# Pooled attention and two feed-forward layers on one core: Float32 heads spread over the second batch, first loads in pieces, the fourth batch's sums inverted by DRAM

## The chip, the cores and the metric

The kernel runs on one core of one Trainium2 chip. The metric is the device time in microseconds (us), the median over runs. The profile is of one such execution and has its own time.

## What is computed

The queries of each of 4 batches and 8 heads (1152 rows of 64) are pooled in pairs, the softmax attention over 1152 keys is taken, and the result goes through two feed-forward layers.

```python
q_pool = q.reshape(B, H, S // factor, factor, D).mean(axis=3)
scores = scale * np.matmul(q_pool, k.transpose(0, 1, 3, 2))
attn = np.exp(scores - np.max(scores, axis=-1, keepdims=True))
attn = attn / (np.sum(attn, axis=-1, keepdims=True) + 1e-09)
x = np.matmul(attn, v)                   # then (tokens, 512)
h = np.maximum(x @ w_in, 0.0)            # first layer, d_ff 2048
x = (s * (h * h) + b) @ w_out
out = (1 / (1 + np.exp(-(x @ w_gate))) * (x @ w_val)) @ w_out2   # second, d_ff 1536
```

The weights arrive as float64 and are decoded on the chip. Matmul operands are split into a high and a low part of type fp32r, and each product is the sum of two or three matmuls of such parts.

## The kernel before

**A plan sets the order.** Every operation is added to a `Plan` (line 1700 on) with its engine, a duration, what it reads and writes, and a rank. `Plan.order` then issues, engine by engine, the free operation with the lowest rank. The rank is the operation's place in its stage, from the tables `ATTENTION` and `FEED`, and a correction from the table `MOVED`, by the operation's name, its pair and its batch. So the order of the instructions on each engine (PE, DVE, ACT, POOL) and of the DMA issues (SP) is fixed at build time, and a number in `MOVED` moves instructions. An engine runs its own list in that order. An operation that either of two engines may do (`shared`) goes to the one that the plan finds free.

**The stages.** For each batch the heads are taken in four pairs. `pair_prep` (L2378) loads q, k and v of a pair, adds the pooled rows of q (L2023), copies the sum beside itself (L2013 on ACT, L2015 on POOL), transposes q and k on PE (L2423), and writes the high parts on ACT (q L2443, k L2020) and the low parts on DVE (q L2446, k L2026). The first batch is done by rows (`pair_rows`): scoring matmuls of 384 keys (L2657), the row maximum of each on DVE (L2664) and of three of them (L2667), the exponential on ACT (L2671), transposes of the probabilities (L2702), and values times probabilities (L2724). The other batches go by half heads (`pair_half`): scoring matmuls (L2493), a running maximum on DVE, transposes of the maximum, a reduce to `mc` (L2510), transposes of that back into rows (L2467), the subtraction, the exponential, and values times probabilities.

**Values times probabilities.** A half head has three thirds of 864 columns. In most heads each third is split into a high and a low part (`split_p`: the high part a cast on ACT, L2013, or POOL, the low part a subtraction, L2023, on DVE or POOL). The heads listed in `WHOLE` (heads 0 to 3 of the second batch) skip the split and use Float32 matmuls (L2549) on the probabilities and values themselves.

**The sums.** Each half head pair needs the reciprocal of 2x288 sums. In `pair_half` (L2617) either the sums are spread to all 64 rows of each half and DVE inverts the 128x288 tile (L2628), or `inverse` writes one row per head to DRAM (L2604), reads it back as 64x9 (L2606), inverts that (L2607), and goes out and back by DRAM (L2608, L2612), all four DMAs on SP. The fourth batch and the last half of each batch's last pair take the first way.

**The feed-forward work of a batch** runs beside the attention of the next one: `ffn1` (`yy` and `xx` are split inputs; its matmuls are L2096 to L2098) and `ffn2`. Those of the fourth batch run at the end, alone. The weights are decoded during the first batch's feed-forward work (`raw`, L2043 to L2059) and fetched from DRAM later (L2073, L2078).

**The PSUM banks.** All PSUM tiles are one of 8 banks. An operation that writes a bank waits until its last reader is done.

Of the kernel before, what the change touches and what calls it, by code (L numbers as in the profile page):

```python
# [3018 lines left out]
```

## Time and profile before

| | |
|---|---|
| median of 3 runs | 1350.54 us (1350.36 to 1352.05) |
| the profiled execution's own time | 1351.29 us |
| its span, first to last instruction | 1349.5 us |
| PE busy | 1313.8 us (97%) |
| DVE busy | 1128.4 us (84%) |
| ACT busy | 903.6 us (67%) |
| POOL busy | 903.2 us (67%) |
| mean granted TensorE clock | 0.996 |

The span is read by engines: an engine's busy time is the time in which one of its instructions ran, and the rest of the span it waited. In a row of the timeline the bracket at the end gives the idle time before the row and what ended it. The granted clock is a share of full speed: 1.00 is the level of 2.4 GHz, 0.50 that of 1.2 GHz.

### The profile page before, as it was taken

The page shows a single profiled execution, that of the slowest core. Times are in us where ns is not written, and L with a number is a line of the kernel's source. Part 1 is how long each engine was busy: PE and PEld are TensorE (multiplying, and loading weights), DVE is VectorE, ACT ScalarE, POOL GpSimd, SP SyncE. Part 2 cuts the span into 40 slices and gives each one's busy share as a digit, 9 for nine tenths or more (in the row PEclk, how much of TensorE's full clock was granted, in tenths as well). Part 3 has the DMA queues.
Part 4 walks back from the last instruction along what each step waited for, and adds up shares of the span by engine and source line. Part 5 has one row for each costly group of instructions (what it writes and reads, how often), then busy time and mean ns, then how long its engine had stood idle before and what let it go on. Part 6 is the DMA issues. An engine that isn't in the chain of part 4 may idle for free.

```text
span 1349.5 us, 21795 instructions
## 1 busy us (share of the span) xinstructions
PE 1313.8 (97%) x7524; PEld 1169.8 (87%) x7524; DVE 1128.4 (84%) x1848; ACT 903.6 (67%) x1919; POOL 903.2 (67%) x767
## 2 busy tenths in 40 slices
PE   7999999998999999999999999999999999999998
PEld 6888888887888898888888888888888899999997
DVE  6899887998989998889989998898978646677675
ACT  6899977667888688768777667676855364343321
POOL 4578755657789876668868877586765455446562
PEclk9999999999999999999999999999999999999999
DMA  3246325876776764445343544343333434435332
GB/s 97 54 116 216 99 90 178 280 243 222 229 259 222 265 198 163 147 160 184 131 144 137 174 165 156 148 161 142 117 143 121 159 132 159 153 120 188 125 125 47
DMA packets 102373, 214.85 MB, mean 159 GB/s; under 512 B 49756, under 2 KB 72056, under 8 KB 86136
## 3 DMA queue, kind: packets, MB, share of 16 engines
q1 hardware_dynamic: 101096, 213.18, 47.4%
q8 instruction: 59, 0.97, 0.3%
q14 instruction: 50, 0.41, 0.1%
q10 hardware_dynamic: 1168, 0.29, 0.1%
HBM read 173.02 MB, written 40.43 MB: 158 GB/s over the span
## 4 chain that ended last, share of the span: by engine, by line
PE 78%; DVE 8%; ACT 6%; POOL 3%; DMA 3%; issue 2%; DVEq 0%; POOLq 0%; ACTq 0%
PE banks L2096 11%; PE banks L2098 11%; PE banks L2097 11%; PE banks L2493 6%; PE banks L2849 4%; PE banks L2851 4%; PE banks L2850 4%; PE banks L2567 3%; PE banks L2233 3%; PE banks L2235 3%; PE banks L2234 3%; PE banks L2559 2%; PE banks L2724 2%; PE banks L2549 2%; DVE st L2026 2%
## 5 line engine op out<-in xcount | busy, mean ns | idle before, releaser
L2026 DVE TENSOR_TENSOR st<-banks,st 128x288 f32<-128x288 f32 x384 | 171.9, 450 | 29.9 <-ACT st L2020 18.2
L2096 PE MATMUL banks<-xx,w 128*128 128x512 f32 x480 | 192.9, 402 | 0.9 <-DVE raw L2059 0.8
L2097 PE MATMUL banks<-xx,w 128*128 128x512 f32 x480 | 188.8, 393 | 0.0
L2098 PE MATMUL banks<-xx,w 128*128 128x512 f32 x480 | 188.8, 393 | 0.0
L2023 POOL TENSOR_TENSOR pp<-st,pp 128x864 fp32r<-128x864 f32 x76 | 173.3, 2285 | 12.2 <-ACT pp L2013 6.0
L2020 ACT COPY st<-banks 128x288 f32<-128x288 f32 x432 | 153.6, 407 | 40.8 <-PE banks L2493 29.9
L2493 PE MATMUL banks<-qT,kT 128*128 128x288 f32 x864 | 158.6, 303 | 2.5 <-DVE y L2340 1.1
L2026 DVE TENSOR_TENSOR st<-st,banks 128x864 f32<-128x864 f32 x144 | 148.2, 1043 | 4.3 <-PE banks L2467 3.9
L2493 PEld LDWEIGHTS banks<-qT,kT 128*128 128x128 f32 x864 | 134.3, 190 | 15.1 <-DVE st L2026 1.4
L2519 ACT ACTIVATE st<-st 128x864 f32<-128x864 f32 x144 | 132.7, 935 | 19.4 <-DVE st L2026 18.3
L2098 PEld LDWEIGHTS banks<-xx,w 128*128 128x128 f32 x480 | 90.5, 189 | 20.1
L2096 PEld LDWEIGHTS banks<-xx,w 128*128 128x128 f32 x480 | 90.7, 189 | 13.2 <-DVE raw L2059 1.0
L2097 PEld LDWEIGHTS banks<-xx,w 128*128 128x128 f32 x480 | 90.9, 189 | 10.8
L2013 ACT CAST pp<-st 128x864 fp32r<-128x864 f32 x102 | 93.4, 922 | 0.8 <-PE banks L2567 0.4
L2096 PE MATMUL banks<-g,w 128*128 128x512 f32 (+2 forms) x256 | 87.4, 342 | 0.0
L2097 PE MATMUL banks<-g,w 128*128 128x256 f32 (+1 forms) x256 | 86.5, 338 | 0.0
L2098 PE MATMUL banks<-g,w 128*128 128x512 f32 (+2 forms) x256 | 86.5, 338 | 0.0
L2023 POOL TENSOR_TENSOR g<-raw,g 128x512 fp32r<-128x512 f32 (+1 forms) x31 | 54.4, 1754 | 37.4 <-ACT g L2013 18.1
L2023 POOL TENSOR_TENSOR w<-raw,w 128x512 fp32r<-128x512 f32 x55 | 75.2, 1368 | 4.9 <-ACT w L2013 4.0
L2023 POOL TENSOR_TENSOR pp<-st,st 128x864 f32<-128x864 f32 x19 | 39.6, 2083 | 43.3 <-ACT st L2519 38.8
L2023 DVE TENSOR_TENSOR pp<-st,pp 128x864 fp32r<-128x864 f32 x44 | 65.6, 1490 | 2.9 <-PE banks L2559 1.1
L2567 PE MATMUL banks<-pp,vt 128*128 128x288 f32 x360 | 67.9, 297 | 0.0
(250 smaller groups left out, 3991.8 us busy)
## 6 DMA issues: line engine op xcount, KB each, us to landing
w<-d_2g_2v SPq DMA_DIRECT2D x26, 1024.0 KB
w<-d_1u_1u SPq DMA_DIRECT2D x24, 1024.0 KB
w<-d_1d_1d SPq DMA_DIRECT2D x24, 1024.0 KB
w<-d_2d_2d SPq DMA_DIRECT2D x18, 1024.0 KB
raw<-in_moe_w_out_dram SPq DMA_DIRECT2D x28, 512.0 KB
d_2g_2v<-w SPq DMA_DIRECT2D x12, 1024.0 KB
w<-d_2g_2v SPq DMA_DIRECT2D x20, 512.0 KB
qn<-in_q_dram SPq DMA_DIRECT2D x16, 576.0 KB
```

The lines of the kernel that those rows point to most:

```text
L2013: nc.scalar.copy(out=out(), in_=in_())
L2020: act(name, n, lambda: nc.scalar.copy(out=out(), in_=in_()), r, w, rank, sbuf=False)
L2023: shared(name, n, lambda e: ENGINE[e].tensor_tensor(out=out(), in0=in0(), in1=in1(), op=op), r, w, rank, 2.25)
L2026: dve(name, n, lambda: nc.vector.tensor_tensor(out=out(), in0=in0(), in1=in1(), op=op), r, w, rank)
L2096: nc.tensor.matmul(ps(), lhsT=whi(), rhs=xhi(), start=first, stop=False)
L2097: nc.tensor.matmul((ps_lo or ps)(), lhsT=whi(), rhs=xlo(), start=False, stop=False)
L2098: nc.tensor.matmul(ps(), lhsT=wlo(), rhs=xhi(), start=False, stop=last)
L2493: nc.tensor.matmul(ps.t[:, :HQ], lhsT=kT.t[:, c], rhs=qq[:, w, hf * HQ:(hf + 1) * HQ], start=(w == 0), stop=(w == 1))
L2519: act("exp", 3 * HQ, lambda s=s: nc.scalar.activation(out=s.t[:, :3], in_=s.t[:, :3], func=AF.Exp), [], parts, AT)
L2567: nc.tensor.matmul(acc.t[:, :HQ], lhsT=vt.t[:, 3 * i + c, cols], rhs=lo.t[:, c], start=False, stop=(i == c == 2))
L2849: nc.tensor.matmul(po.t, lhsT=hi, rhs=w.t[:, 0], start=(i == 0), stop=False)
L2850: nc.tensor.matmul(po.t, lhsT=hi, rhs=w.t[:, 1], start=False, stop=False)
```

## The change

Four parts:

- **Float32 heads.** `WHOLE` lists heads 0, 2, 4 and 6 of the second batch, not 0 to 3. The number of such heads stays 4.
- **First loads.** For the first pair alone, q comes in two loads (of 4 and 5 double rows) and each head's k in two (of 4 and 5 chunks). The first parts of both heads' k are issued by ACT, the rest by SP, q first. The pooled add and the copy beside it are made for each part. Ahead of all that PE gets 13 transposes of the identity (`warm`).
- **The fourth batch's sums.** All its half pairs but the last pair's two are inverted by DRAM.
- **The tables.** `ATTENTION`, `FEED` and nearly all numbers of `MOVED` are new, so instructions move on every engine.

```diff
-WHOLE = [(1, h) for h in range(4)]
+WHOLE = [(1, h) for h in range(0, 8, 2)]
...
-ATTENTION = (0.0, 158.683, 461.124, 811.569, 1195.188)
-FEED = ((143.971, 478.863), (483.888, 862.257), (845.806, 1213.263), (1049.765, 2170.948))
+ATTENTION = (0.0, 157.746, 450.031, 812.875, 1178.305)
+FEED = ((143.343, 476.347), (521.404, 861.584), (845.878, 1191.044), (992.951, 2301.912))
...
-    "q load": 72.917,
...
+    "warm": 94.003,
...
+        first = b == hp == 0
+
+        def warm(count, reads, writes):
+            pt = bank(tag)
+
+            def issue():
+                for i in range(count):
+                    nc.tensor.transpose(pt.t[:, i % 4 * P:(i % 4 + 1) * P], ident, ident)
+
+            pe("warm", count * 107, issue, reads, [pt, *writes], rq - 500)
+
+        if first:
+            warm(13, [], [])
+        rcuts, kcuts = ([(0, 4), (4, RQ)], [(0, 4), (4, NK)]) if first else ([(0, RQ)], [(0, NK)])
...
+        for i in range(len(rcuts)):
+            load_q(i)
+            for j in range(2):
+                load_k(i, j, nc.scalar if first and i == 0 else nc.sync)
...
-        last = b == B - 1 or hp == NP - 1 and hf == 1
+        last = hp == NP - 1 and (b == B - 1 or hf == 1)
```

The count of instructions stays: 7380 matmuls and transposes on PE before, 7393 with the 13 new ones. On DVE six reciprocals of 128x288 become six of 64x9, and SP has 30 more DMA issues for them.

**Where instructions move.** First, PE at the start of the program (`kn` and `qn` are the loaded k and q, `kT` and `qT` their transposed parts, `qm` the middle block of q, `st` the probabilities). Before:

```order
L2423 MATMUL banks<-ident,kn_179 128x128 x9
L2423 MATMUL banks<-ident,qn_182 128x128 x9
L2657 MATMUL banks<-kT_187,qT_208 128x384 x22
L2702 MATMUL banks<-ident,st_237 128x128
L2702 MATMUL banks<-ident,st_248 128x128
```

Changed:

```order
L2405 MATMUL banks<-ident 128x128 x13
L2462 MATMUL banks<-ident,qn_204 128x128 x4
L2462 MATMUL banks<-ident,kn_206 128x128 x4
L2462 MATMUL banks<-ident,qn_204 128x128 x5
L2462 MATMUL banks<-ident,kn_206 128x128 x5
L2696 MATMUL banks<-kT_221,qT_214 128x384 x8
L2696 MATMUL banks<-kT_221,qm 128x384 x2
L2696 MATMUL banks<-kT_222,qm 128x384 x2
```

The transposes come in four parts, q's first part ahead, and all 18 still stand before the first scoring matmul.

Second, DVE at the same place (`sg` holds the row maxima). Before, from the pooled add on:

```order
L2023 TENSOR_TENSOR qn_182<-qn_182 128x9x64
L2026 TENSOR_TENSOR kT_187<-banks,kT_187 64x512
L2026 TENSOR_TENSOR kT_188<-banks,kT_188 64x512
L2026 TENSOR_TENSOR kT_187<-banks,kT_187 64x512
L2026 TENSOR_TENSOR kT_188<-banks,kT_188 64x512
L2026 TENSOR_TENSOR kT_187<-banks,kT_187 64x128
L2446 SCALAR_TENSOR_TENSOR qT_208<-banks,qT_208 128x256
L2446 SCALAR_TENSOR_TENSOR qT_209<-banks,qT_209 128x256
L2446 SCALAR_TENSOR_TENSOR qT_208<-banks,qT_208 128x256
L2446 SCALAR_TENSOR_TENSOR qT_209<-banks,qT_209 128x256
L2026 TENSOR_TENSOR kT_188<-banks,kT_188 64x128
L2664 TENSOR_REDUCE sg_238<-banks 128x1 x4
```

Changed, behind the add of q's first part:

```order
L2485 SCALAR_TENSOR_TENSOR qT_214<-banks,qT_214 128x256
L2485 SCALAR_TENSOR_TENSOR qT_215<-banks,qT_215 128x256
L2039 TENSOR_TENSOR kT_221<-banks,kT_221 64x512
L2039 TENSOR_TENSOR kT_222<-banks,kT_222 64x512
L2485 SCALAR_TENSOR_TENSOR qm<-banks,qm 128x64 x2
L2485 SCALAR_TENSOR_TENSOR qT_214<-banks,qT_214 128x256
L2485 SCALAR_TENSOR_TENSOR qT_215<-banks,qT_215 128x256
L2039 TENSOR_TENSOR kT_221<-banks,kT_221 64x512
L2039 TENSOR_TENSOR kT_222<-banks,kT_222 64x512
L2039 TENSOR_TENSOR kT_221<-banks,kT_221 64x128
L2039 TENSOR_TENSOR kT_222<-banks,kT_222 64x128
L2703 TENSOR_REDUCE sg_261<-banks 128x1 x8
```

All low parts, the middle block's two as well, now stand before the first row maximum, and eight maxima stand before the first maximum of three (the row behind the last one shown), where there were four.

Third, PE at the eighth half head of the second batch, where the first batch's first layer ends and its second begins (`g` and `xx` are inputs of the feed-forward matmuls, `w` weights, `mc` the reduced maximum). Before:

```order
L2098 MATMUL banks<-g_3541,w_3554 128x258
L2423 MATMUL banks<-ident,kn_2995 128x128
L2506 MATMUL banks<-ident,st_3659 96x128 x3
L2493 MATMUL banks<-qT_3756,kT_3810 128x288 x4
L2096 MATMUL banks<-xx_3906,w_3675 128x512
L2097 MATMUL banks<-xx_3906,w_3675 128x512
L2098 MATMUL banks<-xx_3906,w_3675 128x512
L2467 MATMUL banks<-ident,mc_3995 128x96 x3
L2493 MATMUL banks<-qT_3756,kT_3810 128x288 x6
```

Changed:

```order
L2109 MATMUL banks<-g_3664,w_3749 128x258
L2110 MATMUL banks<-g_3664,w_3749 128x256
L2111 MATMUL banks<-g_3664,w_3749 128x258
L2506 MATMUL banks<-ident,mc_3968 128x96 x3
L2532 MATMUL banks<-qT_3851,kT_3901 128x288 x8
L2109 MATMUL banks<-xx_4027,w_3835 128x512
L2110 MATMUL banks<-xx_4027,w_3835 128x512
L2111 MATMUL banks<-xx_4027,w_3835 128x512
L2532 MATMUL banks<-qT_3851,kT_3901 128x288 x2
```

Before, 7 matmuls stand between the transposes of the maximum (L2506) and those of `mc` (L2467). In the change the transposes of the maximum (now L2545) lie 99 matmuls ahead of those of `mc` (now L2506), 96 of them feed-forward matmuls on `g`.

## Rows read from the trace of the kernel before

**Rows 1.** Part 1 of the page: engine, busy us, share of the span, instructions.
```profile
PE 1313.8 (97%) x7524; PEld 1169.8 (87%) x7524; DVE 1128.4 (84%) x1848; ACT 903.6 (67%) x1919; POOL 903.2 (67%) x767
```
**Rows 2.** Windows by stage: us, busy by engine, granted clock, DMA share, GB/s.
```profile
50.00:150.00 100.00, 91.60 (x622) 81.85 (x620) 92.60 (x207) 90.42 (x260) 81.09 (x95) 0.98 0.46 144
150.00:350.00 200.00, 192.56 (x1189) 169.62 (x1188) 172.76 (x342) 145.84 (x318) 123.48 (x148) 0.98 0.59 189
350.00:1050.00 700.00, 694.18 (x3862) 600.47 (x3861) 628.25 (x942) 516.92 (x1023) 526.08 (x377) 1.00 0.50 170
1050.00:1349.50 299.50, 294.86 (x1595) 281.05 (x1593) 197.92 (x274) 112.39 (x210) 151.45 (x114) 1.00 0.39 132
```
**Rows 3.** Windows around two of three stretches at the lower clock.
```profile
121.00:124.20 3.20, 1.41 (x10) 1.17 (x8) 2.91 (x5) 3.12 (x10) 2.95 (x5) 1.00 1.05 238
124.20:127.60 3.40, 3.40 (x19) 3.35 (x19) 3.18 (x8) 2.22 (x7) 2.67 (x4) 0.50 0.44 102
...
332.40:335.80 3.40, 1.59 (x12) 1.10 (x11) 3.03 (x9) 2.94 (x7) 1.93 (x3) 1.00 0.68 149
335.80:339.20 3.40, 3.40 (x14) 3.11 (x13) 3.32 (x7) 2.54 (x7) 2.86 (x4) 0.50 0.74 188
```
**Rows 4.** Timeline, 0 to 20 us: start, us, engine, line, tiles, count, idle before.
```profile
0.74 0.64 ACTq L2390 DMA_DIRECT2D kn<-in_k_dram  x1
...
2.71 0.20 ACT L1945 ACTIVATE early<-values 128x1 f32<-128x1 f32 x1
...
5.65 2.15 PE L2423 MATMUL banks<-ident,kn 128*128 128x128 f32 x9 [5.65 <-DMA kn<-in_k_dram]
6.78 1.77 ACT L2020 CAST kT<-banks 64x512 fp32r<-64x512 f32 x3 [3.87 <-PE banks L2423]
7.80 0.76 DVE L2023 TENSOR_TENSOR qn<-qn 128x576 f32<-128x576 f32 x1 [5.45 <-DMA qn<-in_q_dram]
...
8.59 3.12 DVE L2026 TENSOR_TENSOR kT<-banks,kT 64x512 fp32r<-64x512 f32 x5
...
9.37 2.18 PE L2423 MATMUL banks<-ident,qn 128*128 128x128 f32 x9 [1.56 <-POOL qn L2015]
10.52 0.66 ACT L2443 ACTIVATE qT<-banks 128x256 fp32r<-128x256 f32 x2
...
11.74 1.42 DVE L2446 SCALAR_TENSOR_TENSOR qT<-banks,qT 128x256 fp32r<-128x256 f32 x4
...
12.22 3.79 PE L2657 MATMUL banks<-kT,qT 128*128 128x384 f32 x13 [0.35 <-DVE qT L2446]
...
13.52 1.95 DVE L2664 TENSOR_REDUCE sg<-banks 128x1 f32<-128x384 f32 x4
...
15.69 0.58 ACT L2671 ACTIVATE st<-banks,sg 128x384 f32<-128x384 f32 x1 [3.42 <-DVE sg L2667]
```
**Rows 5.** Timeline of PE, 118 to 124 us.
```profile
119.05 1.20 PE L2423 MATMUL banks<-ident,kn 128*128 128x128 f32 x9 [0.24 <-ACT st L2671]
...
122.92 1.26 PE L2724 MATMUL banks<-g,vt 128*128 128x320 f32 x7 [1.79 <-DVE kT L2026]
```
**Rows 6.** Timeline of PE, 333 to 345 us.
```profile
335.45 0.46 PE L2467 MATMUL banks<-ident,mc 96*128 96x96 f32 x3 [1.81 <-DVE mc L2510]
```
**Rows 7.** Groups of DVE by line and shape, whole run: count, busy us, mean ns, idle before.
```profile
L2023 DVE TENSOR_TENSOR pp<-st,pp 128x864 fp32r<-128x864 f32 x44 | 65.6, 1490 | 2.9 <-PE banks L2559 1.1 <-POOL u L2023 0.7 <-ACT pp L2013 0.4
...
L2628 DVE RECIPROCAL s<-s 128x288 f32<-128x288 f32 x10 | 19.5, 1949 | 0.7 <-ACT s L2586 0.6
```
**Rows 8.** The same view of POOL, its costliest group.
```profile
L2023 POOL TENSOR_TENSOR pp<-st,pp 128x864 fp32r<-128x864 f32 x76 | 173.3, 2285 | 12.2 <-ACT pp L2013 6.0 <-PE banks L2559 2.6 <-POOL pp L2023 1.3
```
**Rows 9.** Waits of PE, 350 to 1060 us: total us, times, longest.
```profile
PE banks L2580 <- DVE u L2023: 1.8, 2, 1.2
```
**Rows 10.** Timeline of SP's queue, 570 to 615 us: one inversion by DRAM.
```profile
573.56 0.50 SPq L2604 DMA_DIRECT2D s_d<-s  x1
...
585.87 1.09 SPq L2612 DMA_DIRECT2D s<-r_d  x2
```

More of the change, by code (lines that the diff above doesn't have):

```diff
@@ new lines @@
+    "warm": 94.003,
+    "warm 1": 94.361,
+    "warm 2": 95.335,
+    "first": 169.513,
+    "first 0": 277.962,
+    "first 1": 262.57,
+    "first 2": 300.879,
+    "v load": 314.208,
+    "v load 0": 183.331,
+    "v load 2": 133.036,
+    "v load 3": 179.221,
+    "v hi": 97.887,
+    "v hi 0": 136.704,
+    "v lo": -97.145,
+    "v lo 0": -29.816,
+    "v lo 1": 87.312,
+    "v lo 3": -55.458,
+    "first q add": 48.26,
+    "first q add 0": 99.331,
+    "first q add 1": 156.132,
+    "first q add 3": 93.082,
@@ new lines @@
+    "first q twice": 337.515,
[662 rows of a table added]
+    "column sum :0": 27.828,
+    "column sum :0 0": 23.493,
+    "column sum :0 1": 13.018,
+    "column sum :0 3": 54.544,
+    "ff y add :0": -94.226,
+    "ff y add :0 0": -121.609,
+    "ff y add :0 1": -270.731,
+    "ff y add :0 3": -106.052,
+    "one :1": 33.594,
+    "one :1 0": 115.065,
+    "one :1 1": 114.394,
+    "one :1 2": 45.246,
+    "ff xx up :1": 0.519,
+    "ff xx up :1 1": -2.765,
+    "ff xx up :1 2": 24.083,
+    "ff xx up :1 3": -547.206,
@@ new lines @@
+    "max @0 2": -26.43,
+    "max rows @0": -458.59,
+    "max rows @0 0": -722.526,
+    "max rows @0 2": -901.766,
+    "max rows @0 3": -1102.635,
+    "s - max @0": 934.659,
+    "s - max @0 0": 790.708,
+    "s - max @0 1": 1063.677,
+    "s - max @0 2": 661.23,
+    "exp @0": 709.509,
+    "exp @0 0": 678.6,
+    "exp @0 1": 372.342,
+    "exp @0 2": 557.84,
+    "pv whole @0": -0.827,
+    "pv whole @0 1": 0.107,
+    "pv whole @0 2": -1.757,
+    "pv whole @0 3": 107.374,
+    "sums @0": -135.076,
@@ new lines @@
+    "max rows @1 2": -508.399,
+    "max rows @1 3": -713.979,
+    "s - max @1": 326.605,
+    "s - max @1 0": 178.091,
+    "s - max @1 1": 470.745,
+    "s - max @1 2": 397.589,
+    "exp @1": 600.733,
+    "exp @1 0": 707.574,
+    "exp @1 1": 260.731,
+    "exp @1 3": 547.406,
+    "pv whole @1": 26.026,
+    "pv whole @1 0": 4.475,
+    "pv whole @1 1": 13.25,
+    "pv whole @1 3": 14.225,
+    "sums @1": -117.13,
+    "sums @1 0": -74.478,
+    "sums @1 2": -219.932,
+    "sums @1 3": -81.402,
@@ new lines @@
+    "1 / sums spread @3 3": -149.514,
+    "1 / sums out @3": 16.226,
+    "1 / sums out @3 0": 19.252,
+    "1 / sums out @3 2": 20.999,
+    "1 / sums out @3 3": 9.222,
+    "1 / sums in @3": -12.632,
+    "1 / sums in @3 1": 66.564,
+    "x / sums @3": 5.0,
+    "x / sums @3 2": -18.673,
+    "1 / sums @3": 21.305,
+    "1 / sums @3 0": 53.171,
+    "1 / sums @3 2": -45.839,
+    "1 / sums @3 3": -45.973,
+    "w fetch :0": -89.168,
+    "w fetch :0 0": -105.609,
+    "w fetch :0 1": 47.102,
@@ new lines @@
+    "p sum chunk @0 0": 38.646,
+    "p sum chunk @0 1": 123.226,
+    "p sum chunk @0 2": 79.495,
+    "p sum hi @0": 2.435,
+    "p sum hi @0 2": -1.422,
+    "p sum lo @0": -10.585,
+    "p sum lo @0 2": -66.627,
+    "all sums @0": -14.578,
+    "all sums @0 0": -12.23,
+    "all sums @0 1": -106.383,
+    "all sums @0 3": 22.332,
+    "x add @0": 66.952,
+    "x add @0 0": 91.289,
+    "x add @0 1": 172.327,
+    "p sum @1": 46.025,
+    "p sum @1 0": 54.167,
+    "p sum @1 2": 33.676,
+    "p sum @1 3": 32.185,
@@ new lines @@
+    "p sum chunk @1": -823.076,
+    "p sum chunk @1 0": -203.821,
+    "p sum chunk @1 1": -113.79,
+    "p sum chunk @1 3": -227.805,
+    "p sum hi @1": 58.448,
+    "p sum hi @1 0": 12.91,
+    "p sum hi @1 2": 2.123,
+    "p sum hi @1 3": 111.875,
+    "p sum lo @1": -56.444,
+    "p sum lo @1 0": -42.03,
+    "p sum lo @1 1": -23.252,
+    "p sum lo @1 3": -23.27,
+    "all sums @1": -56.539,
+    "all sums @1 0": -54.536,
+    "all sums @1 1": -21.175,
+    "all sums @1 3": -55.106,
+    "x add @1": -54.9,
@@ new lines @@
+    "all sums @2": -29.265,
+    "all sums @2 0": 12.727,
+    "all sums @2 1": -58.558,
+    "all sums @2 2": 12.949,
+    "x add @2": 12.396,
+    "p sum @3": 5.77,
+    "p sum chunk @3": -24.41,
+    "p sum chunk @3 0": -20.9,
+    "p sum chunk @3 2": 18.865,
+    "p sum chunk @3 3": -22.317,
+    "p sum hi @3": 54.692,
+    "p sum hi @3 0": 278.037,
+    "p sum hi @3 2": 282.22,
+    "p sum hi @3 3": 267.062,
+    "p sum lo @3": -34.227,
+    "p sum lo @3 2": -36.777,
+    "p sum lo @3 3": 52.647,
@@ new lines @@
+    "yy S lo :1 3": -128.203,
+    "p2 yy up :1": 68.371,
+    "p2 yy up :1 1": -26.681,
+    "p2 yy up :1 2": 31.016,
+    "p2 yy up :1 3": -58.327,
+    "p2 yy up :2": -79.701,
+    "p2 yy up :2 0": -302.176,
+    "p2 yy up :2 2": -87.446,
+    "p2 yy up :2 3": -73.438,
+    "w fetch half :2": 100.315,
+    "w fetch half :2 2": 114.623,
+    "W whole :2": 89.39,
+    "W whole :2 0": 38.257,
+    "W whole :2 1": -11.378,
+    "W whole :2 3": 9.774,
+    "T :2": 137.773,
+    "T :2 1": 193.24,
@@ new lines @@
+    "p2 B22 :2 2": 59.804,
+    "p2 B22 :2 3": 66.151,
+    "w fetch half :3": -127.023,
+    "w fetch half :3 0": -210.054,
+    "w fetch half :3 2": -143.635,
+    "w fetch half :3 3": -142.999,
+    "W whole :3": 152.413,
+    "W whole :3 0": 113.185,
+    "W whole :3 1": 83.721,
+    "W whole :3 3": 39.1,
+    "T :3": -128.293,
+    "T :3 1": -240.017,
+    "T :3 2": -149.882,
+    "T :3 3": -221.229,
+    "T hi :3": -183.727,
+    "T hi :3 1": -121.049,
+    "T hi :3 2": -181.054,
+    "T hi :3 3": -268.751,
@@ L2429, in pair_prep @@
             n = min(4, RQ - r0)
-            pt = transposed(f"{tag} qT", r0, n, lambda r: qn.t[:, 2 * r:2 * r + 2].rearrange("p a d -> p (a d)"), [qn], qT)
+            pt = transposed(f"{tag} qT", r0, n, lambda r: qn.t[:, 2 * r:2 * r + 2].rearrange("p a d -> p (a d)"), [(qn, int(first and r0 > 0))], qT)
             def view(j, pt=pt, n=n):
@@ L2450, in pair_prep @@
             n = min(4, NK - c0)
-            pt = transposed(f"{tag} kT", c0, n, lambda c: kn.t[:, c].rearrange("p h d -> p (h d)"), [(kn, 0), (kn, 1)], kT)
+            pt = transposed(f"{tag} kT", c0, n, lambda c: kn.t[:, c].rearrange("p h d -> p (h d)"), [(kn, j, int(first and c0 > 0)) for j in range(2)], kT)
             for j in range(2):
```

1808 lines of the change are left out of this document (827 added, 981 removed), and 1329 rows, old and new, of the table MOVED.

## The prediction

> **What bounds the kernel now.** I read the page's engine totals first. PE is busy 1313.8 us of a span of 1349.5 [rows 1], so all its idle time is 35.7 us, and no other engine comes near that share. As the change leaves the number and shapes of PE's instructions alone, but for 13 early transposes, it can win only from that idle time and from time in which PE runs slower than it could.
>
> The windows by stage say where this time lies [rows 2]. From 350 to 1050 us PE is busy 694.18 of 700 us, and behind 1050 us it idles 4.6 us, which is the tail after the last matmul. Between 50 and 150 us it idles 8.4 us and from 150 to 350 us 7.4 us. The rest, 35.7 - 5.8 - 4.6 - 8.4 - 7.4 = 9.5 us, is before 50 us, and 5.65 us of that is the wait for the first k [rows 4]. So behind 350 us PE is saturated: whatever ends earlier there shifts the end one for one, and what DVE, ACT or POOL save there shifts nothing unless PE waits for it.
>
> The second loss is the clock. In the stretches at 124.2 and 335.8 us the granted clock is 0.50, the 1.2 GHz level, and each follows a window in which PE was busy less than half (1.41 of 3.20, 1.59 of 3.40) [rows 3]; a third of the same kind lies at 254 us. PE is busy throughout such a stretch and gets half done, so each costs up to 3.4 / 2 = 1.7 us.
>
> At the start the rows show a slow PE too. Nine transposes take 2.15 us at 5.65 us and 2.18 us at 9.37 us [rows 4], and 1.20 us at 119.05 us [rows 5]: 0.24 against 0.13 us each.
>
> **The sum, against the profiled execution's 1351.29 us.**
>
> *Start.* What must be there for the first exponential is q and k transposed, split, scored, and three row maxima. Before, PE's first transposes start at 5.65, the stream of scoring matmuls at 12.22, the first exponential at 15.69 us [rows 4]. In the change q's first part is ahead, but the second head's first part of k is issued by ACT behind the table load and the activation that ends at 2.71 + 0.20 = 2.9 us, where the load on ACT was issued at 0.74 before [rows 4]. The rows show no landing of so small a load. It lies between 5.65 (it is 4/9 of a head, and the loads of 0.7 us had landed whole by then) and 5.65 + 2.2 = 7.8 us (shifted by the later issue); I take 6.3, nearer the first because fewer bytes are ahead. By the order, PE then has 4 + 5 + 5 transposes before the first score: 14 x 0.24 = 3.4, so 9.7 us. Meanwhile ACT casts two k parts (0.59 each [rows 4], to 7.3 + 1.2 = 8.5) and DVE takes their low parts (0.62 each, to some 9.7). So the scoring stream starts 12.22 - 9.7 = 2.5 us earlier.
>
> ACT then has four casts of q (0.33 each, to 9.8) and four of k (two of 0.59, two small, to some 11.5), and DVE's last low part ends at about 12.1 us. DVE does eight maxima (1.95 / 4 = 0.49 each) before the first maximum of three, where it did four: 12.1 + 3.9 + 0.2 = 16.2, so the first exponential comes 0.5 us later than now. At that time, though, DVE has eight maxima behind it where it now has five (four by 15.47, then one each 0.49): 3 x 0.49 = 1.5 us ahead. The term lies between -2.5 and +0.5 us. I take -1.0, near DVE's lead less the later exponential, since every later block needs its maxima. I price all transposes here at the slow pace.
>
> The 13 warm-up transposes run while PE waits for data and cost nothing: 13 x 0.24 = 3.1 us fit before 5.65 us, as the identity needs no load. If it were late, the 14 transposes behind them would be late by what is over.
>
> The Trainium skill speaks against their use: in "TensorE: Matmul & The Clock Gate", section "Part 4: PE-mode transpose", it says that the full clock does not engage for transposes. The trace agrees as far as it goes, since the second nine transposes were as slow as the first nine [rows 4]; by the opposite rule the term would be -2.5 instead of -1.0.
>
> *Place at 121 us.* PE idled 1.79 us in front of values times probabilities, waiting for DVE's low parts of k, with nine transposes of k and eight of q just ahead [rows 5]; these hold banks that only DVE and ACT free. The slow stretch followed [rows 3]. In the new order nine transposes stand there and q's nine come 16 rows later. The price is 1.79 + 1.7 = 3.5 us at most. But DVE is busy 92.6 and ACT 90.4 of 100 us between 50 and 150 us, and there is no feed-forward work yet that PE could put in the gap. I take -0.5, between 0 and -3.5, near 0 for that reason.
>
> *Place at 333 us.* PE idled 1.81 us for the reduced maximum `mc` [rows 6], and then ran 3.4 us at the lower clock [rows 3]. Only 7 matmuls covered the reduce. In the new order 96 feed-forward matmuls of the first layer lie in between, so this wait is gone. What is late next is the last quarter of the first layer's output y, which must be added, biased and split before the second layer's fourth group of matmuls; 8 + 2 + 2 scoring matmuls and three groups stand ahead of it. There is matmul work behind, and PE is saturated from 350 us on [rows 2], so what is saved here stays saved. The price is 1.81 + 1.7 = 3.5 us. I take -2.5, the whole wait and nearly half the slow stretch; the ends are -3.5 and 0.
>
> *Fourth batch's sums.* DVE loses six reciprocals of 1.95 us each [rows 7], 11.7 us, and gets six on a 32nd of the columns. ACT writes as long a row as before. But DVE's time counts only where PE waits for DVE, and the waits behind 350 us are few: the largest group has 1.8 us [rows 9], all of PE's idle time there is 5.8 us. Against that, SP gets 30 more issues. One inversion takes from 573.56 to 585.87 + 1.09 us, 13.4 us from end to end [rows 10], and what is queued behind a waiting issue on SP are weight fetches. Fourteen such chains run now in the second and third batches beside a PE that is busy 99%, so that cost is hidden by fetches made ahead; were this cover gone, each chain might hold a fetch by a few us. The divided x is needed by the last feed-forward stage alone. I take -0.5, between -2 and +1.5.
>
> *Float32 heads.* As many as before, so PE's work is equal. Four half heads' worth of splitting moves into 150 to 350 us, and as much out of what follows. That is 4 x 3 = 12 thirds, each a low part of 2.29 us on POOL [rows 8] or 1.49 on DVE [rows 7]. POOL is busy 123 and DVE 173 of 200 us there [rows 2]: 12 x 2.29 = 27 us fit on POOL. I take 0, between -2 (PE waits less behind) and +6 (below).
>
> *The rest of the tables* moves instructions everywhere; the trace of before cannot show their waits. I take 0.
>
> Sum: -1.0 - 0.5 - 2.5 - 0.5 = -4.5, so 1346.8 us against the profile's own 1351.29. The median of the runs is 0.75 us below that execution, so the forecast for the median is **1346.0 us**, with a range of its own of 1343.0 to 1347.8.
>
> **The rivals.**
>
> *Nothing is won.* The late y takes the place of the late `mc`, with its slow stretch, and the loads in pieces come no earlier, since ACT's second issue is late. For it: the first exponential is not earlier by my own working, and DVE is nearly full until 350 us. Against: 96 matmuls are a lot of cover. Then only -1.0 is left, 1349.5 us, between 1347.8 and 1353.2. Chance 0.28.
>
> *More is won.* The tables also clear half of PE's other idle time between 50 and 350 us, (8.4 + 7.4) / 2 = 7.9 us (the two places above are within it), besides the start's -1.0: 1341.6 us. For it: the idle time consists of many small waits that an order can cover. Against: before 150 us DVE and ACT are full. Chance 0.18.
>
> *The warm-up works*, and PE is at full pace from the first k on: the 14 transposes are 14 x (0.24 - 0.13) = 1.5 us shorter, -2.5 in place of -1.0 at the start, 1344.5 us. Against: the 18 slow transposes of now. Chance 0.06.
>
> *Slower: the split low parts.* In 150 to 350 us the weights are decoded, with low parts of the same kind on POOL and DVE. Where the 12 thirds land on POOL while DVE is full, each third holds PE's product with it by 2.29 - 1.49 = 0.8 us or more, up to 12 x 0.8 = 9.6 us; with half of that uncovered and one more slow stretch it is 4.8 + 1.7 = 6.5, against -1.5 won at start and end: 1355.5 us. It decides from the point where PE finds no feed-forward matmul to put before the product. Against: POOL's 77 free us there. Chance 0.14.
>
> **How the numbers follow.** About 0.2% (2.7 us) is what a measurement of this kernel can tell from no change: faster is below 1347.8, slower above 1353.2. My forecast has 0.34. Faster: 0.34 + 0.18 + 0.06 = 0.58. Same: 0.28. Slower: 0.14. The range reaches from the larger gain to the end of the case without one, 1340.5 to 1353.0; it leaves out the slower case and the far end of the larger gain.
>
> **What would show it.** In the profile after, the first scoring matmul should start at 9 to 10.5 us and the first exponential at 15.5 to 17. The wait for `mc` at the end of the first layer should be gone, and the stretches at clock 0.50 be two or fewer. PE's busy time from 350 to 1050 us should stay above 693 of 700 us, with no wait for sums or weight fetches in the last third. The prediction is wrong if PE's idle time between 150 and 350 us grows beyond 9 us (then the split heads or the y chain), if PE waits for DMAs of weights behind 800 us (the inversions), or if the start's first exponential comes before 15 us (then the pieces give more than I think).

## The result, and the profile after

The changed kernel takes **1359.8 us** (median of 4 runs, 1356.3 to 1360.8) against 1350.45 of the kernel before: a ratio of **1.0062, interval 1.0038 to 1.0086**. Run again among the experiments it took 1356.7 us, 1.0039 (1.0027 to 1.0052). It is slower by 5 to 9 us, where 4.5 us less was forecast. The profiled execution has 1356.32 us, the shortest of its four, and a span of 1354.5, 5.0 above before.

The engine totals of the changed kernel (first part of the page):

```profile
PE 1315.5 (97%) x7537; PEld 1165.9 (86%) x7537; DVE 1134.1 (84%) x1855; ACT 910.0 (67%) x1926; POOL 896.8 (66%) x753
```

PE's idle time is 1354.5 - 1315.5 = 39.0 us, 3.3 more than before [rows 1]; its busy time grew by 1.7, with the 13 warm-up transposes (3.03 us) in it. The windows by stage of the changed kernel (columns as in [rows 2]):

```profile
0.00:16.00 16.00, 11.25 (x53) 9.22 (x53) 10.05 (x23) 6.83 (x16) 6.48 (x15) 1.00 0.74 184
16.00:50.00 34.00, 29.97 (x203) 26.65 (x204) 25.44 (x59) 29.90 (x93) 15.95 (x23) 0.95 0.18 49
50.00:150.00 100.00, 89.25 (x613) 77.48 (x612) 91.66 (x203) 89.33 (x255) 78.10 (x91) 1.00 0.44 141
150.00:350.00 200.00, 193.18 (x1258) 172.44 (x1257) 179.94 (x351) 161.69 (x348) 139.12 (x149) 1.00 0.59 189
350.00:1050.00 700.00, 692.04 (x3792) 594.39 (x3791) 621.83 (x947) 508.62 (x1005) 496.53 (x362) 1.00 0.50 168
1050.00:1354.50 304.50, 299.79 (x1626) 285.73 (x1624) 205.17 (x277) 113.61 (x212) 160.60 (x116) 1.00 0.40 138
```

Against [rows 2], PE idles 2.3 us more from 50 to 150 us, 0.6 less from 150 to 350, 2.1 more from 350 to 1050. DVE did lose its 11.7 us of reciprocals, but its total is higher than before. The start (timeline; us, duration, engine, line; in the changed kernel a line of the functions stands 39 further down, so L2703 is L2664 and L2710 is L2671, and a line of the helpers 13, so L2039 is L2026):

```profile
1.68 3.03 PE L2405 MATMUL banks<-ident 128*128 128x128 f32 x13 [1.68 <-POOL ident masks.py:199]
...
7.71 0.71 PE L2462 MATMUL banks<-ident,kn 128*128 128x128 f32 x5
8.99 1.14 PE L2696 MATMUL banks<-kT,qT 128*128 128x384 f32 x5 [0.56 <-DVE kT L2039]
...
12.80 3.81 DVE L2703 TENSOR_REDUCE sg<-banks 128x1 f32<-128x384 f32 x8
13.40 0.51 PE L2696 MATMUL banks<-kT,qT 128*128 128x384 f32 x2
16.64 0.16 DVE L2706 TENSOR_REDUCE sg<-sg 128x1 f32<-128x3 f32 x1
16.84 0.58 ACT L2710 ACTIVATE st<-banks,sg 128x384 f32<-128x384 f32 x1 [2.87 <-DVE sg L2706]
...
17.56 1.25 PE L2696 MATMUL banks<-kT,qT 128*128 128x384 f32 x3 [3.64 <-ACT st L2710]
```

The scoring starts at 8.99 us, 3.2 earlier than before [rows 4], but the first exponential is at 16.84, 1.15 later. By 13.9 us PE has filled eight tiles, one for each of DVE's eight maxima and as many as there are banks, and then it waits 3.64 us for that exponential. The granted clock of that stretch and the next (windows):

```profile
13.90:17.70 3.80, 0.16 (x2) 0.14 (x2) 2.87 (x7) 0.93 (x4) 2.07 (x2) 1.00 0.18 67
17.80:21.20 3.40, 3.23 (x10) 2.35 (x10) 2.20 (x6) 2.82 (x11) 0.00 (x0) 0.50 0.31 87
```

**Where the time went.** To compare orders, each of PE's matmul records was given the median spacing of its kind in the trace of before, and the sum taken as work done. Both traces hold the same 7524 records (7380 instructions, of which the 144 Float32 matmuls that are no transposes leave two each), beside the 13 warm-up transposes, which count as none. The table says how many us later than before a kernel reaches the same work (less: earlier), in its one profiled execution.

| before, at us | 46 | 105 | 196 | 247 | 301 | 357 | 408 | 459 | 535 | 1320 |
|---|---|---|---|---|---|---|---|---|---|---|
| changed kernel | 2.2 | 5.2 | 5.6 | 6.4 | 5.5 | 2.0 | 3.4 | 4.7 | 4.8 | 4.9 |
| the same, second profile | 3.4 | 6.3 | 8.5 | 9.9 | 8.6 | 4.5 | 5.9 | 7.0 | 7.3 | 7.5 |
| loads in pieces alone (e1) | 3.1 | 3.0 | 3.0 | 2.4 | 0.5 | -1.2 | -1.2 | -0.9 | -0.9 | -1.3 |
| warm-up alone (e4) | 0.5 | 1.1 | 1.3 | 1.2 | 1.2 | -1.9 | -2.0 | -1.7 | -1.7 | -1.7 |
| sums alone (e8) | 0.3 | 0.3 | 1.5 | 1.3 | 1.3 | -0.2 | -0.2 | 0.5 | 0.6 | -0.6 |
| change, old loads (e2) | 7.3 | 9.6 | 11.5 | 11.9 | 10.7 | 8.7 | 10.6 | 11.8 | 12.0 | 11.9 |
| heads alone (e5) | -0.3 | -0.2 | 0.2 | 2.0 | 4.4 | 2.7 | 4.9 | 8.2 | 8.3 | 8.0 |
| all but heads and first orders (e9) | 2.7 | 2.7 | 2.6 | 1.5 | 0.4 | -1.0 | 0.9 | 1.1 | 0.6 | 1.0 |
| head 3 to 4 alone (e10) | 0.2 | 0.2 | 2.3 | 3.0 | 2.6 | 1.9 | 5.0 | 6.8 | 7.4 | 11.7 |
| heads, order searched (e13) | -2.0 | 2.0 | 1.2 | 0.9 | -2.0 | -4.3 | -3.3 | -3.3 | 1.2 | -0.8 |
| change's parts, order of e13 (e17) | 0.1 | 2.6 | 1.4 | 1.9 | -1.3 | -3.2 | -2.4 | -2.2 | 3.2 | 3.0 |
| e13 with warm-up and sums (e18) | -0.3 | 3.6 | 3.0 | 3.5 | 0.5 | -1.4 | -0.6 | -0.5 | 2.4 | 0.1 |

The changed kernel loses 5 us by 105 us, wins 3.5 back between 301 and 357, and loses 2.7 again by 459 us, in waits of up to 0.5 us each. Behind 535 us nothing is lost. Every row is measured against one execution of before and carries what that one lost: it ran 3.4 us at clock 0.50 behind 254 us, as the prediction names it, and again behind 336 [rows 3]. So e4 and e8, which keep the order of before there, win 3.1 and 1.5 us between 301 and 357 as well, and beside these two only 0.4 to 2.0 of the changed kernel's 3.5 are its own.

### The profile page after: what moved, and what is told of

It reads as the page before. It is cut to its first block, busy times and chain, and to the rows that moved or that the text cites. A ratio compares the mean times of both kernels' runs of the same rounds, so it can differ in the third digit from the quotient of the medians.

```text
span 1354.5 us, 21869 instructions
## 1 busy us (share of the span) xinstructions
PE 1315.5 (97%) x7537; PEld 1165.9 (86%) x7537; DVE 1134.1 (84%) x1855; ACT 910.0 (67%) x1926; POOL 896.8 (66%) x753
## 4 chain that ended last, share of the span: by engine, by line
PE 72%; DVE 10%; ACT 6%; DMA 4%; POOL 4%; issue 3%; SPq 0%; DVEq 0%; POOLq 0%; ACTq 0%
PE banks L2109 10%; PE banks L2110 10%; PE banks L2111 10%; PE banks L2532 6%; PE banks L2888 3%; PE banks L2890 3%; PE banks L2889 3%; PE banks L2246 3%; PE banks L2606 3%; PE banks L2248 3%; PE banks L2247 3%; PE banks L2598 2%; DMA raw<-in_moe_w_out_dram 2%; DMA raw<-in_moe_w_val_dram 2%; DVE st L2039 2%
## 5 line engine op out<-in xcount | busy, mean ns | idle before, releaser
L2039 DVE TENSOR_TENSOR st<-banks,st 128x288 f32<-128x288 f32 x384 | 172.3, 451 | 33.4 <-ACT st L2033 17.5
L2036 POOL TENSOR_TENSOR pp<-st,pp 128x864 fp32r<-128x864 f32 x72 | 165.7, 2305 | 18.7 <-ACT pp L2026 8.8
L2039 DVE TENSOR_TENSOR st<-st,banks 128x864 f32<-128x864 f32 x144 | 148.6, 1043 | 5.9 <-PE banks L2506 5.7
L2026 ACT CAST pp<-st 128x864 fp32r<-128x864 f32 x105 | 96.6, 922 | 6.0 <-PE banks L2598 3.3
L2036 POOL TENSOR_TENSOR w<-raw,w 128x512 fp32r<-128x512 f32 x59 | 79.1, 1347 | 10.7 <-ACT w L2026 9.7
L2036 POOL TENSOR_TENSOR pp<-st,st 128x864 f32<-128x864 f32 x23 | 49.9, 2169 | 50.5 <-ACT st L2558 31.8
L2036 DVE TENSOR_TENSOR pp<-st,pp 128x864 fp32r<-128x864 f32 x48 | 74.0, 1542 | 3.6 <-ACT pp L2026 3.0
L2710 ACT ACTIVATE st<-banks,sg 128x384 f32<-128x384 f32 x108 | 63.0, 599 | 13.1 <-DVE sg L2706 12.9
```

Source lines behind the costliest of these rows:

```text
L2026: nc.scalar.copy(out=out(), in_=in_())
L2036: shared(name, n, lambda e: ENGINE[e].tensor_tensor(out=out(), in0=in0(), in1=in1(), op=op), r, w, rank, 2.25)
L2039: dve(name, n, lambda: nc.vector.tensor_tensor(out=out(), in0=in0(), in1=in1(), op=op), r, w, rank)
L2710: act("r exp", 384 + 224, lambda c=c, ps=ps: nc.scalar.activation(out=p.t[:, c * 384:(c + 1) * 384], in_=ps.t[:, :384], func=AF.Exp, bias= ...
```

## The experiments

Many experiments must alter one thing and leave the order alone, though the plan would re-plan everything. In these, each operation's rank is the time at which the plan of the *named* kernel issues it (a table `PIN`), and an operation of two engines keeps its engine:

```diff
         key = self.here + rank + self.moved.get(self.named(name), 0.0)
+        pinned = PIN.get(f"{self.stage}|{name}")
+        if pinned:
+            key, on = pinned.pop(0)
+            self.on[i] = [on]
```

What is kept is the rank. The plan still issues the free operation with the lowest one, so the order follows only as far as the edit lets it. The longest sequence of PE records, by tile and shape, that a run has in common with before is 7522 of 7524 in e4, 7426 in e8, 7065 in e10 and 6971 in e5, where the moved heads' own products are 180 of the 553 that are missing. Operations that the named kernel lacks have no place in the table and go by the old ranks: the first pair's whole loads and their pooled sum in e2, the splits of the second batch's values in e5, e6, e10 and e11. Kernels that ran together share the runs of before (their medians: 1350.2 for e1 to e4, 1349.7 for e5 to e8, 1350.5 for e9 to e12, 1351.5 for e13 to e16, 1349.8 for e17 and e18).

| run | us | ratio to before, interval |
|---|---|---|
| e1 new start alone | 1351.9 | 1.0013 (0.9999 to 1.0026) |
| e2 change, old start | 1360.1 | 1.0073 (1.0057 to 1.0089) |
| e3 change, first batch in old order | 1359.5 | 1.0077 (1.0063 to 1.0090) |
| e4 warm-up alone | 1349.6 | 0.9996 (0.9986 to 1.0007) |
| e5 heads alone | 1363.5 | 1.0094 (1.0072 to 1.0115) |
| e6 change, old heads | 1366.8 | 1.0123 (1.0103 to 1.0142) |
| e7 change, old sums | 1358.8 | 1.0063 (1.0047 to 1.0079) |
| e8 sums alone | 1349.7 | 0.9999 (0.9989 to 1.0010) |
| e9 all but heads and first orders | 1351.6 | 1.0006 (0.9992 to 1.0020) |
| e10 head 3 to 4 | 1360.3 | 1.0078 (1.0057 to 1.0099) |
| e11 head 1 to 6 | 1363.1 | 1.0102 (1.0082 to 1.0123) |
| e12 warm-up and sums | 1347.6 | 0.9982 (0.9963 to 1.0001) |
| e13 heads, order searched | 1350.5 | 0.9991 (0.9980 to 1.0001) |
| e14 change, order searched | 1359.0 | 1.0052 (1.0036 to 1.0067) |
| e15 warm-up, sums, order searched | 1356.4 | 1.0030 (1.0019 to 1.0041) |
| e16 change again | 1356.7 | 1.0039 (1.0027 to 1.0052) |
| e17 change's parts, order of e13 | 1355.3 | 1.0042 (1.0025 to 1.0059) |
| e18 e13 with warm-up and sums | 1352.0 | 1.0012 (0.9995 to 1.0029) |

**The start: e1 to e4.** e1 puts the new loads and `warm` into the kernel before, pinned to before's order; e2 takes them out of the changed kernel, pinned to its own; e3 pins the attention of the first batch in the changed kernel to before's order; e4 adds the warm-up alone to before. The edits of e3 and e4, beside the pinning (`P_old`, `P_new` are the places in the two kernels):

```diff
-PIN = P_new
+PIN = {k: P_old[k] if k.startswith("0|") and ":" not in k else P_new[k] for k in P_new}
...
+        if b == hp == 0:
+            warm(13, [], [])
```

> The kernel before with the loads in pieces and the 13 warm-up transposes, everything else issued in the order of before (the ranks are the places of before's own order, so DVE does four maxima before the first maximum of three). Pieces theory (the loads in pieces themselves lose the time): first exponential at 16.8 us, the lag of about 3 us of the changed kernel at 60 us appears here, 1353 to 1354 us. Order theory (the new order of the first batch loses it): full clock from 7.5 us on, first exponential at 13.5 to 14.5 us, 1347 to 1349.5 us.

> The changed kernel with the loads of before (whole, no warm-up), everything else in its own new order, in which DVE does eight maxima before the first maximum of three. Pieces theory: 3 us better than the changed kernel, 1356 to 1357 us. Order theory: no better, or 1 to 3 us worse, 1360 to 1363 us.

> The changed kernel, all four of its parts, with the first batch's attention issued in the order of before and the rest in its own new order. Order theory: the lag of 3 to 5 us at 100 us is gone, 1354 to 1356.5 us. Late theory (the time is lost from the second batch on, by the Float32 heads and the order there): 1358.5 to 1361 us as the changed kernel, the lag appearing behind 160 us.

> The kernel before with the 13 warm-up transposes alone, loads whole, order of before. If the warm-up lifts the clock early: granted clock 1.0 before 8 us where it rose at 14.96 us, the 18 transposes of k and q in 2.4 us instead of 4.3, 0.5 to 1.5 us less, 1349 to 1350 us. If transposes don't lift it: nine transposes of k in 2.15 us as before, 1350.5 us.

The timeline of e1 (its scoring is L3555, its exponential L3569):

```profile
9.74 2.11 PE L3555 MATMUL banks<-kT,qT 128*128 128x384 f32 x8
...
13.37 1.95 DVE L3562 TENSOR_REDUCE sg<-banks 128x1 f32<-128x384 f32 x4
...
15.54 0.58 ACT L3569 ACTIVATE st<-banks,sg 128x384 f32<-128x384 f32 x1 [3.34 <-DVE sg L3565]
...
16.27 2.00 PE L3555 MATMUL banks<-kT,qT 128*128 128x384 f32 x6 [2.19 <-ACT st L3569]
```

Even in the old order the loads in pieces bring PE's scoring forward by 2.5 us and the first exponential by 0.15 us only: DVE's maxima begin at 13.37, behind the low parts. PE stands 2.19 us with full banks, and 6.8 us at clock 0.50 follow: it is 3.1 us behind at 46 us. By 357 us its row shows this lag gone, and its median lies between the two theories, so neither holds for e1. That the lag was regained isn't shown, however: of the 3.6 us between 247 and 357, e4 and e8 win 3.1 and 1.5 too.

e2 has the time of the order theory, and without the pieces the new order is 7.3 us behind at 46 us. But its start isn't clean: its load of q is issued fourth on SP, at 2.96 us (before: second, at 1.50), and POOL adds the pooled rows at 9.60 us (before: DVE at 7.80), so its transposes of q start at 11.76 us, where before's started at 9.37 [rows 4]. Its median is only 0.3 to 3.4 us above the changed kernel's (its profiled execution, the longest of its six, keeps its lag).

e3 came out as the late theory has it, but its lag grows from 3.9 to 9.0 us between 105 and 196 us, around where its two orders meet, so it isn't clean. What stands is that the loads in pieces bring PE's scoring forward without the exponential, and that the old order in the first batch alone, with the new one behind it, repairs nothing. In e4 the clock did not rise early (the last section shows it), and the warm-up alone gains nothing that can be measured.

**The heads and the sums: e5 to e8.** e5 changes `WHOLE` alone in the kernel before, pinned: whole products take the ranks of the old split ones and the reverse, new splits stand 4 us ahead of their products, on a free engine. e6 does the reverse in the changed kernel. e7 and e8 exchange the one line of `last`, pinned. The edits of e5 and e8 (e6 and e7 are the reverse, in the changed kernel):

```diff
-WHOLE = [(1, h) for h in range(4)]
+WHOLE = [(1, h) for h in range(0, 8, 2)]
...
-        last = b == B - 1 or hp == NP - 1 and hf == 1
+        last = hp == NP - 1 and (b == B - 1 or hf == 1)
```

> The kernel before with the Float32 heads alone moved (heads 0, 2, 4, 6 for 0 to 3 of the second batch); loads, sums and the order of everything else as before, the changed heads' products in the places of the old ones and their splits 4 us ahead. Heads theory (the spread heads lose the time, split low parts between 150 and 350 us): PE falls behind before by 5 us or more from 160 us on and does not regain it, 1356 to 1360 us. Table theory (the spread is free, only the new numbers lose): 1350 to 1352 us.

> The changed kernel with the Float32 heads of before (0 to 3), the rest in its own order, the changed heads' products in the places of the old ones. Heads theory: 4 to 8 us less than the changed kernel, 1351 to 1355 us. Table theory: no less, 1359 to 1363 us.

> The changed kernel with the fourth batch's sums inverted by DVE as before (six reciprocals of 128x288 back, 24 DMA issues fewer), the rest in its own order. If the inversions by DRAM lose time: 2 to 6 us less than the changed kernel, 1354 to 1357 us, the difference appearing behind 800 us. If they cost nothing: as the changed kernel, 1358 to 1361 us, and PE at the same distance from before at 800 us and at the end.

> The kernel before with the fourth batch's sums alone inverted by DRAM. If the inversions lose time: 1353 to 1356 us, lost behind 800 us. If they cost nothing: 1350 to 1350.5 us. If DVE's 11.7 us count: 1348 to 1349.5 us.

The sums cost nothing and win nothing, alone or taken back (the trace of the changed kernel has 30 issues more on SP, not the 24 of e7's expectation). Moving the heads with the ranks of before costs 13.9 us, more than the heads theory had, from 247 us on and not from 160; some of PE's waits in e5 from 150 to 470 us, the three largest first (waits; L3406 is the whole product, L3418 the high and L3424 the low part of the split one), and its windows:

```profile
PE banks L3406 <- ACT st L3376: 4.0, 2, 2.2
PE banks L3418 <- ACT pp L2870: 2.3, 1, 2.3
PE banks L2954 <- POOL xx L2880: 2.1, 2, 1.6
...
PE banks L3424 <- POOL pp L2880: 0.8, 2, 0.4
```

```profile
150.00:350.00 200.00, 189.42 (x1217) 168.13 (x1216) 173.35 (x339) 148.94 (x321) 142.18 (x154) 0.99 0.58 188
350.00:1050.00 700.00, 689.57 (x3783) 592.87 (x3781) 625.55 (x938) 506.00 (x1009) 503.08 (x366) 1.00 0.49 166
```

PE idles 3.1 us more than in [rows 2] in the first stretch and 4.6 more in the second. But e6 is slower than the changed kernel too, by 7 to 10 us: the *old* heads in the new order cost as well. That fits neither theory. What e5 and e6 share is that the ranks were made for other heads.

**Which part of the order: e9 to e12.** e9 is the new start and sums with the old heads; attention of the first two batches and the first feed-forward work are pinned to before, the rest to the changed kernel. e10 and e11 are e5 with one head moved. e12 is e4 and e8 together. The edits of e9, e10 and e11:

```diff
-PIN = P_new
+PIN = {k: P_old[k] if k[0] == "0" or k[0] == "1" and ":" not in k else P_new[k] for k in P_new}
...
-WHOLE = [(1, h) for h in range(4)]
+WHOLE = [(1, h) for h in (0, 1, 2, 4)]
...
-WHOLE = [(1, h) for h in range(4)]
+WHOLE = [(1, h) for h in (0, 2, 3, 6)]
```

> New loads in pieces, warm-up, the new sums of the fourth batch, and the changed kernel's order for everything from the second feed-forward work on (third and fourth batch, feed-forward work of the second to fourth); Float32 heads, both first batches and the first batch's feed-forward work in the order of before. If heads and order of the first two batches are the whole loss: 1349.5 to 1352.5 us, PE level with the new start alone behind 460 us. If the late order loses too: 1354 us or more, with PE falling behind after 500 us.

> The kernel before with one Float32 head moved: heads 0, 1, 2, 4 of the second batch for 0 to 3. If each moved head costs the same, half of what both cost: about 7 us, 1356 to 1358 us. If the loss is at one place that head 4 makes (a whole product that waits for its exponential at 268 us): 1354 to 1356 us. If only the last pair matters: 1350 to 1351.5 us.

> The kernel before with the other Float32 head moved: heads 0, 2, 3, 6 for 0 to 3, so head 1 is split in the first pair and head 6 is whole in the last. If each moved head costs the same: 1356 to 1358 us. If the last pair makes the loss (waits at 407 to 416 us): 1354 to 1356 us, lost behind 400 us. If the first pair makes it (one split head more while the weights are decoded): lost at 160 to 230 us.

> The kernel before with the two parts that cost nothing alone, the warm-up transposes and the fourth batch's sums by DRAM, in the order of before; loads whole, heads 0 to 3. If their small gains add up: 1348.5 to 1349.5 us. If neither is a gain: 1350 us.

e9 is level with before: the new loads, the sums and the new order behind the second batch are free together. The loss lies in the heads and the order of the first two batches together; e9 exchanges both. e10 and e11 cost 10 and 13 us, above all that was expected, and with both moves e5 costs 13.9, not their sum: it is no price per head. Nor does it all arise in the second batch: of the 11.7 us that e10's profiled execution (the longest of its five) is behind, 4.3 come behind 535 us. e12 is 0.18% below before, lower than either of its expectations, with an interval that just takes in 1: not shown to be a gain.

**Heads or order: e13 to e18.** e13 is e5 with its order up to 480 us searched anew: ranks shifted at random, and engines of `shared` operations exchanged, a shift kept where the plan's own last operation ends earlier. e14 and e15 search the whole program's order in the same way, from that of the changed kernel and from that of e12. e16 is the changed kernel. e17 is its code with the order of e13, e18 is e13 with `warm` and the new `last`. The edits of e13 and e17 (`P_s` is what the search left):

```diff
-PIN = P_old
+PIN = P_s
...
-PIN = P_new
+PIN = P_s
```

> The kernel before with the Float32 heads spread (as in the run with the heads alone) and the order of the first 480 us searched anew: ranks shifted at random, a shift kept where the plan's own last operation comes earlier; loads and sums as before. Heads theory (they lose the time whatever the order): 1358 us or more, PE 5 us or more behind before at 480 us. Order theory (the heads cost nothing where the order fits them): 1349 to 1353 us, PE within 2.5 us of before at 480 us.

> The changed kernel, all four parts, with its order searched anew in the same way, from its own order on. Order theory: a good part of the 9 us comes back, 1351 to 1356 us. Heads theory: 1358 to 1361 us, as the changed kernel.

> The kernel before with the warm-up transposes and the fourth batch's sums by DRAM, heads 0 to 3, whole loads, and its order searched anew in the same way. If the search alone is what wins, and the old order had room left: 1343 to 1347 us. If the order of before was as good as it gets: 1348 to 1351 us.

> The changed kernel unaltered. All theories: 1359 to 1361 us, ratio 1.005 to 1.008; a second profile, with two or three stretches at the lower clock where the first profile had one before the end, if these are why the median lies 3.5 us above the profiled execution.

> The changed kernel's code, all four parts, with the places of its operations taken from the order of the run with the heads in a searched order (behind 480 us that is nearly the order of before); only the order differs from the changed kernel. Table theory (the re-tuned tables are the loss): 1350 to 1353 us, about what the loads in pieces and the sums cost alone. If the parts hurt each other whatever the order: 1356 us or more.

> The kernel before with the spread heads in their searched order, the warm-up transposes and the fourth batch's sums by DRAM; loads whole. If the parts that cost nothing add up to a gain as in the run with warm-up and sums: 1347 to 1349 us, below before. If not: 1350 us.

The same windows for e13:

```profile
150.00:350.00 200.00, 195.74 (x1271) 174.92 (x1270) 180.90 (x354) 155.86 (x335) 145.85 (x158) 1.00 0.58 190
350.00:1050.00 700.00, 691.43 (x3788) 593.76 (x3787) 624.21 (x941) 504.01 (x1006) 497.57 (x362) 1.00 0.50 170
```

With the same heads as e5, PE idles 4.3 us from 150 to 350 us in place of 10.6, and the time is that of before: **the spread heads cost nothing in an order that fits them.** The way there is not even: e13 is 3.3 us ahead at 459 us and 1.2 behind at 535, around where its searched order ends. It is not the search that wins: a search of the same kind, over the whole program, makes e12 worse (e15, against both its expectations; its loss lies behind 790 us, where it is 1.0 us ahead and at the end 5.2 behind) and leaves the changed kernel where it was (e14, where the order theory had hoped for 3 to 8 us).

e17 is a miss. The changed kernel's four parts in e13's order should have come to 1350 to 1353 us and took 1355.3, not clear of the changed kernel. e13's order had been found without the loads in pieces, but the profile doesn't show the loss where these act: at 459 us e17 is 2.2 us ahead of before, where the changed kernel is 4.7 and 7.0 behind. It loses 5.4 us from there to 535, as e13 loses 4.5 and e18 2.9, around where the searched order ends; how much of the lead was work merely done earlier isn't known. What it wins back by 900 us goes again at 911, in a wait of 1.76 us with a stretch at the lower clock behind it. e18, the same without the pieces, is 0.12% above before, with 1 in its interval, and above both its expectations. The intervals of e17 and e18 overlap, so that the pieces cost the 3.3 us between their medians is neither shown nor excluded. So no order was found here in which all four parts together are level with before, and whether there is one stays open.

e16 came out lower than expected, so the changed kernel's loss is nearer 6 than 9 us. Its windows show what goes with the difference between two executions of the changed kernel:

```profile
13.00:17.00 4.00, 1.46 (x8) 1.14 (x7) 3.96 (x9) 0.67 (x1) 1.45 (x2) 0.99 0.55 154
17.00:23.70 6.70, 5.34 (x17) 4.62 (x18) 3.93 (x11) 5.28 (x18) 1.51 (x2) 0.50 0.17 44
187.50:191.00 3.50, 2.23 (x12) 1.51 (x12) 3.43 (x9) 2.59 (x7) 1.62 (x2) 1.00 0.12 46
191.00:194.40 3.40, 3.15 (x10) 2.70 (x11) 3.09 (x6) 1.68 (x2) 0.85 (x2) 0.50 0.00 0
```

The order is the same, but here 6.7 us run at the lower clock after the first wait and 3.4 at 191 us, where the first profile had 3.4 us in all before the end. That is 6.7 us more at half speed, at most 3.4 us, and the spans differ by 2.6.

## Why the prediction was wrong

**The step that failed is the last term:** "The rest of the tables moves instructions everywhere; the trace of before cannot show their waits. I take 0." It was the only term without bounds, and by elimination it held the result: 5 to 9 us slower, where the four priced terms gave 4.5 us less. e9 puts the loss into the order of the first two batches and the heads that go with it, and e13 shows that these heads can be had at the time of before, so the order is left. e5, e6, e10 and e11 show the size that such a term can have: heads that the order wasn't made for cost 0.6 to 1.0%, two to three times everything else in the sum together. It isn't shown directly, as no run with the order alone exchanged comes out level (e14, e17), and what in the order costs the time stays open. That the term reaches further to the slower side could have been seen: from 50 to 350 us PE idled only 15.8 us [rows 2] beside a DVE that was busy 86% and more, so there was little to win and any operand that comes late to lose.

**The start** was forecast at -1.0 us. The scoring came at 8.99 (9.7 forecast) and the first exponential at 16.84 (16.2), so the working held; the weighing failed. "I take -1.0, near DVE's lead less the later exponential, since every later block needs its maxima" set the maxima ready against the exponential late. But here PE, with its eight banks full, could only go on when an exponential had freed one. Its earlier start became a wait of 3.64 us and a slow stretch, +2.2 us at 46 us. In the order of before the part costs 0 to 3.5 us at the end (e1).

**The warm-up** was a rival with a chance of 0.06, and its condition came true in part and in one execution: the last five transposes of k took 0.71 us, 0.14 each, where nine took 2.15 before [rows 4], but most of the 13 ahead of them were slow, and in e16, the same kernel, these five were too (timeline of e16):

```profile
8.41 1.27 PE L2462 MATMUL banks<-ident,kn 128*128 128x128 f32 x5
```

Its price of 1.5 us was not won, as the transposes are not what the first exponential waits for. In e4 they were as slow as ever.

**The place at 121 us** was forecast at -0.5: the wait for k's low parts is gone, but others came, and PE idles 10.75 us from 50 to 150 in place of 8.4. The largest is that of the scoring matmuls for DVE's low parts of the transposed probabilities, here in `g` (waits from 50 to 150 us, before and then the changed kernel):

```profile
PE banks L2724 <- DVE kT L2026: 1.8, 1, 1.8
PE banks L2657 <- DVE g L2026: 1.0, 2, 0.8
```

```profile
PE banks L2696 <- DVE g L2039: 2.8, 3, 1.2
```

**The place at 333 us** lost its wait for `mc` as forecast, and no wait from 300 to 350 us is longer than 0.7 us. The lag falls from 5.5 to 2.0 us, by 3.5 where -2.5 stood, but 0.4 to 2.0 us of that are the change's own (e4 and e8 in the table). In e8, which keeps before's order there, PE waits 1.87 us for the same `mc`, and its clock stays up, where [rows 3] has 0.50:

```profile
333.20:336.70 3.50, 1.63 (x12) 1.14 (x9) 3.13 (x10) 2.63 (x6) 2.02 (x3) 1.00 0.63 144
336.70:340.10 3.40, 3.40 (x21) 3.10 (x22) 3.32 (x8) 3.40 (x9) 3.14 (x4) 1.00 0.66 171
```

One execution's slow stretch was booked as the kernel's. The wait for `mc` is there in e1, e4 and e12 too (1.77, 1.32 and 1.80 us); a stretch at 0.50 follows in e1, and none in e4 and e12.

**The sums** at -0.5 (nothing, e7 and e8) and **the heads** at 0 (nothing where the order fits, e13) were right within what can be measured, the second only with that condition, which the text didn't name.

**The slower rival** (split low parts, 1355.5 us) has nearly the right time by luck, and not the right place. It was to show as idle time of PE above 9 us from 150 to 350; it is 6.8. In e5 that idle time is there, 10.6 us, but its largest waits are for the exponential and the high part's cast on ACT, and those for low parts on POOL come to 0.8 us. None of the three signs of being wrong showed up: besides the idle time, PE waits for no weight fetch behind 800 us, and the first exponential is not before 15 us. "Above 693 of 700 us" for PE's busy time from 350 on failed by a little: 692.04.

## What to carry to other kernels

A re-tuned order is a term of its own, with bounds of its own, and where PE is busy 97% of the span these reach further to the slower side than to the faster: of the runs here the best came to 0.998 of before and the worst to 1.012. To test a part of such a change, hold the order of everything else, and count how much of it was held; what then is lost may still be the misfit of order and part, which only an order made for the part can tell. A lag against one execution carries that execution's own losses, so a row that should be flat belongs beside it. PE's earlier start won nothing here while the exponentials that empty its banks came no earlier.
